# A spectral mixing transform feeding a two-layer expert: the transform in an unbroken turn, its last two batches' inverse kept in DRAM, and the seven-product form of w_out in eleven tiles in place of five

## The chip, the cores and the metric

The kernel runs on one core of a Trainium2 chip. The metric is the device time of one execution in microseconds (us). Three runs of the kernel before gave a median of 2568.8 us (2568.28 to 2569.6).

## What is computed

```python
X = np.fft.rfft(x, axis=1)                      # x: 8 x 3008 x 256
Yr = Xr @ w_r - Xi @ w_i + b_r                  # complex mix of the 256 channels
Yi = Xr @ w_i + Xi @ w_r + b_i
Yr, Yi = softshrink(Yr, 0.01), softshrink(Yi, 0.01)
y = np.fft.irfft(Yr + 1j * Yi, n=3008, axis=1)
h = y.reshape(24064, 256) @ w_in                # 256 x 2048
g = np.maximum(h, 0.0) ** 2
out = g @ w_out                                 # 2048 x 256
```

Everything is float32. The products are done as sums of three products of parts, high by high, low by high and high by low (fp32r), so every product of the algorithm is three matmuls.

## The kernel before

**The expert.** The 24064 tokens are worked in 48 tiles, six to a batch (`tiles`, line 492): tile t belongs to batch t // 6 and has 2h tokens, h being 252 or 250. A tile has eight steps (`Step`, line 690), one for every 256 of the 2048 hidden columns. `first` and `second` (702, 733) make the hidden columns with seven products in place of eight (21 matmuls of h columns, 12 and 9). DVE adds the products up and rectifies them, ACT squares them into `mc` and copies the high part to `mg0`, and POOL subtracts the low part `mg1` in two halves (line 752). `out(0)` and `out(1)` (811) multiply by w_out, two steps later: 6 matmuls of 2h columns each, accumulated over the tile in two PSUM banks `pso`. Only the last two matmuls of each six read `mg1`.

**The seven-product form of w_out.** In tiles named by `FREE` (line 59: 42 to 46) the steps 1, 3 and 5 (`SEVEN`) use seven products for w_out too (`out_seven`, 768): 9 and 12 matmuls of h columns. It needs sums of the hidden columns (`forms`, 755: four on DVE, copies of the high parts on ACT, low parts `ftl` on POOL), sums of w_out made once (`out_sums`, 663, on POOL) and two further PSUM banks of the transform's pair `psf` as accumulators for the rest of the tile; `tile_sums` (678) adds them up on DVE at its end. The memory for this (`LATE`: `wsh`, `wsl`, `tt`, `th`, `tl`, `ts`) lies where the transform of a batch has its tiles (`SIDE`), so `late` (904) opens it once the last batch's forward part and mix are through.

**The transform of the next batches** fills in between the steps. For each batch: 13 `Fwd` (210; short DFTs, stored to DRAM `s1`), 12 `Pair` (267; second DFT, mix, shrink, first inverse stage, stored to `s3`) and 16 `Back` (499; last inverse stage of 188 tokens, 6 matmuls). A `Back` loads its tile `du`, multiplies into two `psf` banks, and ACT and DVE add the two halves into the next tile's raw tokens `yr`. `Tokens` (576) makes the seven sums and low parts `yt` of the tile's tokens, which `first` and `second` read.

**The order of the work** is written by the main loop (1078 to 1131). It counts slots m: step n has slots 2n (`first`) and 2n+1 (`second`); a batch has 96. Transform work hangs on a list of (slot, job): a job is put behind what that slot writes. In the kernel before, the 12 Pairs of a batch stand 6 slots apart in the slots 1 to about 75 of the batch ahead of its use, the 13 Fwd in the slots 4 to 78, and the rest of the 96 has neither. The 16 Backs of a tile's batch run one tile ahead.

A scheduler turns this into one queue per engine, each of which runs in order; earlier written work goes first where it is ready. `then` (572) chains instructions of an engine, so that their order is as written: all matmuls of the steps (`product`, `out`, `out_seven`), DVE's and ACT's parts of the steps, and on POOL the low parts of `mg` and the sums of `Tokens.free`. Loads on SP are chained too (`load_next`, 117). A tile with one buffer (`ts` has one) is given out again only when the last reader of its former holder is done.

**The last batch before the change.** `last_tasks` (897) runs all 16 Backs of batch 7 in the slots 645.5 to 671 of the loop, 1.6 slots apart, with `du` in the tags `th`, `tl`, `th`, `ts` in turn; the last one (q = 15, tag `ts`) loads in slot 666 and multiplies in slot 671. Their results go to DRAM (`y7`), from where `raw_load` (892) brings each tile. The tokens of tile t + 1 are then made inside the steps of tile t in `FREE` by `Tokens.free`, written into the odd slots:

```python
            ahead = k and t in FREE and i in (0, 2, 4, 6)
            if ahead:
                if i == 0:
                    tokens = Tokens(t + 1)
                tokens.free(i, False)
            (steps[n].second if k else steps[n].first)()
```

Its first act is to take the tile `ts` and write two differences into it on POOL (582 to 591), ahead of the low parts of the same step in POOL's chain. For tile 42 that is slot 673.

## Time and profile before

| | |
|---|---|
| median of three runs | 2568.8 us |
| the profiled execution's own time | 2568.52 us |
| its span, first to last instruction | 2566.7 us |
| PE busy | 2557.8 us, 17345 matmuls |
| DVE, POOL, ACT busy | 1864.5, 1711.5, 1405.7 us |
| granted TensorE clock, mean | 1.000 |
| HBM | 96 GB/s over the span |

The profile gives one execution. PE is the matmuls of TensorE, PEld its weight loads, DVE the vector engine, ACT the scalar engine, POOL GpSimd, SP the queue that issues most transfers. Matmuls overlap in the records, each ending after the next has begun, so what one costs is read from start to start. Tile 42 begins at about 2311 us, tile 46 at about 2474 us and the last, 47, at about 2515 us.

### The profile page before, as it was taken

The page shows a single profiled execution, that of the slowest core. Times are in us where ns is not written, and L with a number is a line of the kernel's source. Part 1 is how long each engine was busy: PE and PEld are TensorE (multiplying, and loading weights), DVE is VectorE, ACT ScalarE, POOL GpSimd, SP SyncE. Part 2 cuts the span into 40 slices and gives each one's busy share as a digit, 9 for nine tenths or more (in the row PEclk, how much of TensorE's full clock was granted, in tenths as well). Part 3 has the DMA queues.
Part 4 walks back from the last instruction along what each step waited for, and adds up shares of the span by engine and source line. Part 5 has one row for each costly group of instructions (what it writes and reads, how often), then busy time and mean ns, then how long its engine had stood idle before and what let it go on. Part 6 is the DMA issues. An engine that isn't in the chain of part 4 may idle for free.

```text
span 2566.7 us, 47569 instructions
## 1 busy us (share of the span) xinstructions
PE 2557.8 (100%) x17345; PEld 2361.9 (92%) x17345; DVE 1864.5 (73%) x3727; ACT 1405.7 (55%) x2151; POOL 1711.5 (67%) x1653
## 2 busy tenths in 40 slices
PE   9999999999999999999999999999999999999999
PEld 7899999999999999999999999999999999999998
DVE  7876766777767776687766877677776676667886
ACT  5655555555555555555555555555555455555554
POOL 1167666676767766677667666667777666768885
PEclk9999999999999999999999999999999999999999
DMA  9633332343323333233332333323342223340000
GB/s 313 196 94 90 115 93 83 94 122 106 94 68 106 103 106 96 65 109 103 116 94 70 103 112 109 94 58 113 102 120 76 70 89 103 93 119 31 25 25 17
DMA packets 186608, 249.82 MB, mean 97 GB/s; under 512 B 18616, under 2 KB 131760, under 8 KB 186376
## 3 DMA queue, kind: packets, MB, share of 16 engines
q1 hardware_dynamic: 172961, 221.51, 27.7%
q0 software_dynamic: 13280, 25.16, 4.2%
q8 instruction: 139, 2.28, 0.4%
q14 instruction: 93, 0.76, 0.1%
q10 hardware_dynamic: 135, 0.12, 0.0%
HBM read 146.76 MB, written 99.95 MB: 96 GB/s over the span
## 4 chain that ended last, share of the span: by engine, by line
PE 98%; DVE 1%; DMA 1%; ACT 0%; issue 0%; POOL 0%; SPq 0%; ACTq 0%
PE pso L574 40%; PE psh L574 36%; PE psf L309 7%; PE psf L288 3%; PE psf L342 2%; PE psf L250 2%; PE psf L474 1%; PE psf L552 1%; PE psf L551 1%; PE psf L574 1%; PE psf L548 1%; PE psf L372 1%; PE psf L529 1%; PE psf L409 0%; PE psf L484 0%; PE psf L460 0%
## 5 line engine op out<-in xcount | busy, mean ns | idle before, releaser
L112 POOL TENSOR_TENSOR mg<-mc,mg 128x500 fp32r<-128x500 f32 (+1 forms) x766 | 990.0, 1314 | 485.7 <-ACT mg L108 404.6
L574 PE MATMUL pso<-mg,wout 128*128 128x500 f32 (+2 forms) x4473 | 1128.0, 390 | 0.0
L574 PE MATMUL psh<-yt,win 128*128 128x250 f32 (+1 forms) x8064 | 1070.2, 280 | 0.8 <-DVE mc L574 0.3
L574 PEld LDWEIGHTS psh<-yt,win 128*128 128x128 f32 x8064 | 1018.8, 189 | 29.4 <-DVE yt L112 0.6
L574 PEld LDWEIGHTS pso<-mg,wout 128*128 128x128 f32 x4473 | 798.6, 189 | 126.2
L574 ACT ACTIVATE mc<-mc 128x1000 f32<-128x1000 f32 (+1 forms) x384 | 400.5, 1043 | 494.6 <-DVE mc L574 493.4
L574 DVE CUSTOM_DVE_ANT_0 mc<-psh,mv 128x250 f32<-128x250 f32 (+3 forms) x769 | 418.6, 546 | 336.8 <-PE psh L574 291.6
L108 ACT CAST mg<-mc 128x1000 fp32r<-128x1000 f32 (+1 forms) x385 | 396.7, 1031 | 15.0 <-ACT mc L574 0.4
L574 DVE TENSOR_TENSOR mv<-psh,mu 128x500 f32<-128x500 f32 (+1 forms) x384 | 260.8, 679 | 43.3 <-PE psh L574 8.9
L309 PE MATMUL psf<-wx,kxh 128*128 128x256 f32 x1008 | 209.5, 281 | 0.0
L109 DVE COPY mp<-psh 128x250 f32<-128x250 f32 (+1 forms) x384 | 160.4, 418 | 50.9 <-PE psh L574 27.4
L330 DVE TENSOR_TENSOR kv<-psf,ke 64x256 f32<-64x256 f32 x336 | 141.6, 422 | 46.3 <-PE psf L309 33.5
L221 POOL TENSOR_TENSOR xs<-xt 120x256 f32<-120x256 f32 x156 | 121.2, 798 | 80.0 <-DMA xt<-x_in 41.9
L309 PEld LDWEIGHTS psf<-wx,kxh 128*128 128x128 f32 x1008 | 167.0, 189 | 2.7
L574 DVE TENSOR_TENSOR mu<-psh,mp 128x250 f32<-128x250 f32 (+1 forms) x384 | 160.7, 418 | 12.0
L574 DVE CUSTOM_DVE_ANT_0 mc<-psh,mp 128x250 f32<-128x250 f32 (+1 forms) x384 | 156.9, 408 | 7.1 <-PE psh L574 6.9
L108 ACT COPY dy<-psf 128x188 f32<-128x188 f32 (+2 forms) x229 | 70.2, 317 | 162.4 <-PE psf L552 161.9
L112 POOL TENSOR_TENSOR ksl<-kv,ksh 128x512 fp32r<-128x512 f32 x84 | 109.0, 1297 | 57.7 <-ACT ksh L108 56.2
L309 PE MATMUL psf<-wx,kxl 128*128 128x256 f32 x504 | 141.6, 281 | 0.0
L112 POOL TENSOR_TENSOR yt<-yr,yt 128x250 fp32r<-128x250 f32 (+1 forms) x94 | 88.7, 944 | 46.3 <-ACT yt L108 46.3
L332 ACT ACTIVATE kc<-kv,low 128x512 f32<-128x512 f32 x84 | 60.8, 724 | 100.3 <-DVE kv L330 100.2
L112 DVE TENSOR_TENSOR xl<-xs,xh 120x512 fp32r<-120x512 f32 x78 | 112.4, 1441 | 1.3 <-ACT xh L108 1.3
(163 smaller groups left out, 2883.4 us busy)
## 6 DMA issues: line engine op xcount, KB each, us to landing
du<-s SPq DMA_DIRECT2D x112, 256.0 KB, 2.9
ka<-s SPq DMA_DIRECT2D x96, 256.0 KB, 2.9
kcm<-cm_in POOLq DMA_DIRECT2D x84, 256.0 KB, 3.6
s<-kuh SPq DMA_DIRECT2D x84, 256.0 KB, 2.9
s<-kul SPq DMA_DIRECT2D x84, 256.0 KB, 3.5
s<-xe SPq DMA_DIRECT2D x82, 240.0 KB, 2.4
xt<-x_in SPq DMA_DIRECT2D x81, 240.0 KB, 3.1
out<-mo SPq DMA_DIRECT2D x64, 250.0 KB, 2.3
```

Source lines behind the costliest of these rows:

```text
L108: return act.copy(out=out, in_=in_)
L109: return eng.tensor_copy(out=out, in_=in_)
L112: return eng.tensor_tensor(out=out, in0=a, in1=b, op=ALU.subtract)
L221: return eng.tensor_tensor(out=out[:, :n], in0=self.xt[:, :n, 0], in1=self.xt[:, :n, 1], op=(ALU.add, ALU.subtract)[t])
L250: nc.tensor.matmul(ps[:, t], am_sb[0][:, j, t], v[:, t], start=n == 0, stop=n == 2)
L288: nc.tensor.matmul(pv[:, :, c, g, :], self.a[:, g, c * 128:(c + 1) * 128], bg, start=True, stop=True)
L309: self.last = nc.tensor.matmul(ps, l, wx[j][:, k, c, :], start=n == 0, stop=n == 5)
L330: dve.tensor_add(out=v[64 * r:64 * r + 64, g], in0=ps[gs], in1=self.e[gs, r])
L332: act.activation(r, v, AF.Relu, bias=low)
L342: nc.tensor.matmul(ps[:, g], self.cm[:, g, j * 128:(j + 1) * 128], r[:, g], start=n == 0, stop=n == 2)
L372: self.mm = nc.tensor.matmul(ps[:M1, t], nam if t and i else am32[:, t], self.xt[:, 0, i], start=i == 0, stop=i == 1)
L574: last_of[eng] = op(*args, **kwargs)
```

## The change

`FREE` becomes 36 to 46, and the Backs of batch 6 go to DRAM as those of batch 7 do. The batches from 2 on follow one another every 78 slots (13 turns of 6) from slot 92, in place of every 96: Fwd of batch b + 1 start four slots after batch b's turn, its Pairs seven slots after. All job lists are put together once, in absolute slots. Worked out from the new numbers: the last turn begins in slot 482 and batch 7's Pairs end in 554.25 (`done`); batch 6's Backs run from 488 to 553, 4.2 slots apart, their `du` in the tag `xt`; `late` is in 554.75; batch 7's Backs run from 555.25 to 580.85, 1.6 slots apart as before. The last of them loads in slot 576.05 and multiplies in 580.85. Tile 36 begins in slot 576, and `Tokens.free` for tile 37 first runs in slot 577.

```diff
--- before.py
+++ after.py
@@ -55,7 +55,8 @@
 
 A11, A12, A22, S1, S2, S3, S4 = range(7)
 B11, B21, B22, T1, T3, T2, T4 = range(7)
-ENDS = B - 1
+ENDS = B - 2
+TURN0, TURNS, PACE = 92, J, 6
 FREE = range(ENDS * len(HALF), B * len(HALF) - 1)
 SEVEN = (1, 3, 5)
 
@@ -71,7 +72,7 @@
 
     s3 = [dram.tile([M2 + M2 if b else M2, NP, D], F32, name=f"s3_{b}") for b in range(B)]
 
-    y7 = dram.tile([128, 2, S], F32, name="y7")
+    ys = {b: dram.tile([128, 2, S], F32, name=f"y_{b}") for b in range(ENDS, B)}
 
     am32 = const.tile([M1, 2, M1], F32, name="am32")
     dx_sb = const.tile([128, 2, 4 * N2], F32R, name="dx_sb")
@@ -507,20 +508,25 @@
 
         def load(self):
             tag = "du" if self.spans[0][0] else "mc"
-            if self.b == ENDS:
+            if self.b == B - 1:
                 tag = ("th", "tl", "th", "ts")[self.q % 4]
             ps = slice(2 * self.q, 2 * self.q + 2)
             if self.b == 0:
                 self.u = T("du", [M2, 2, D], F32, tag=tag)
                 load_next(self.u, s3[0][:, ps])
                 return
-            if self.b == ENDS:
-                self.u = T("du", [128, 1024], F32R, tag=tag)[:, :3 * D].rearrange("p (k d) -> p k d", k=3)
+            if self.b == B - 1:
+                u = T("du", [128, 1024], F32R, tag=tag)[:, :3 * D].rearrange("p (k d) -> p k d", k=3)
+                self.u, self.u2 = u[:, :2], u[:, 2]
+            elif self.b >= ENDS:
+                self.u, self.u2 = [T("du", [128, 2, D], F32R, tag="xt") for _ in range(2)]
+                self.u2 = self.u2[:, 0]
             else:
-                self.u = T("du", [128, 3, D], F32R, tag=tag)
-            load_next(self.u[:, :2].bitcast(F32), s3[self.b][:128, ps])
+                u = T("du", [128, 3, D], F32R, tag=tag)
+                self.u, self.u2 = u[:, :2], u[:, 2]
+            load_next(self.u.bitcast(F32), s3[self.b][:128, ps])
             for p in range(2):
-                load_next(self.u[64 * p:64 * p + 64, 2].bitcast(F32), s3[self.b][128:, 2 * self.q + p])
+                load_next(self.u2[64 * p:64 * p + 64].bitcast(F32), s3[self.b][128:, 2 * self.q + p])
 
         def mm32(self):
             ps = bank([128, 512])[:, :2 * W2].rearrange("c (k p t) -> c k p t", k=2, p=2)
@@ -549,17 +555,16 @@
 
                 with tc.issue_after(mm.ins):
                     nc.tensor.matmul(pv[:, :, 1], self.u[:, 1, cs], dx_sb[:, 0], start=False, stop=False)
-                nc.tensor.matmul(ps[:, 0], self.u[:, 2, cs], dx_sb[:, 1], start=False, stop=True)
+                nc.tensor.matmul(ps[:, 0], self.u2[:, cs], dx_sb[:, 1], start=False, stop=True)
                 self.done = copy(act, y[:, c], ps[:, 1])
                 for n, (t, lo, hi, at) in enumerate(self.spans):
-                    kept = t in FREE[1:] or t > FREE[-1]
+                    kept = t >= FREE[0]
                     if n == c == 0 and t not in raw and not kept:
                         raw[t] = T("yr", [128, 2, 2 * HM], F32)
                     o = y[:, c, lo:hi] if n or kept else raw[t][:, c, at:at + hi - lo]
                     self.cut = dve.tensor_add(out=o, in0=ps[:, 0, lo:hi], in1=y[:, c, lo:hi])
-            if self.b == ENDS and self.spans[-1][0] > FREE[0]:
-                lo = min(lo for t, lo, _, _ in self.spans if t > FREE[0])
-                nc.sync.dma_start(y7[:, :, W2 * self.q + lo:W2 * (self.q + 1)], y[:, :, lo:])
+            if self.b >= ENDS:
+                nc.sync.dma_start(ys[self.b][:, :, W2 * self.q:W2 * (self.q + 1)], y)
 
         def put(self):
             t, lo, hi, _ = self.spans[1]
@@ -845,7 +850,7 @@
         jobs = []
         for j, u in enumerate(pairs):
             at = start + j * step
-            if j:
+            if j or u.b > 1:
                 jobs += [(at - 3.7, u.load)]
             jobs += [
                 (at, u.fwd), (at + 1.0, u.sums), (at + 3.7, u.load_back),
@@ -854,21 +859,23 @@
             ]
         return jobs
 
-    def fwd_tasks(b, start, step):
+    def fwd_tasks(b, start):
         jobs = []
-        step0 = (b - 2) * len(HALF) * NF // 2
         for q in range(J):
-            f, at = Fwd(b, q), start + q * step - (step0 > 0 and q == J - 1)
-            add = f.add if q or not step0 else lambda f=f, s=steps[step0 - 1]: later(s.low, f.add)
-            even = 6 * q + (4 if step0 else 14 if q < 4 else 18)
+            f, even = Fwd(b, q), start + PACE * q
+            add = f.add
+            if b > 2 and q == 0:
+                add = lambda f=f, s=steps[(start - 4) // 2 - 1]: later(s.low, f.add)
+            elif b == 2 and q > 3:
+                even += 4
             jobs += [(even - 5.0, f.load), (even - 1.9, add), (even - 0.9, f.split), (even + 0.1, f.lower)]
-            jobs += [(even + (2.0 if step0 else 1.2), f.run)]
+            jobs += [(even + (2.0 if b > 2 else 1.2), f.run)]
         return jobs
 
     def back_tasks(t, start):
         b, c0, h = tiles[t]
         new = range(-(-c0 // W2), -(-(c0 + 2 * h) // W2))
-        if b == ENDS:
+        if b >= ENDS:
             new = ()
         jobs = []
         for j, q in enumerate(new):
@@ -880,6 +887,8 @@
                 jobs += [(start + 14.6, k.put)]
         if t > FREE[0]:
             return [(start, lambda: raw_load(t))]
+        if t == FREE[0]:
+            jobs += [(start, lambda: raw_load(t))]
         k = Tokens(t)
         if t == 0:
             return jobs + [(start + 7.1, k.begin)]
@@ -890,16 +899,16 @@
         return jobs
 
     def raw_load(t):
-        _, c0, h = tiles[t]
+        b, c0, h = tiles[t]
         raw[t] = T("yr", [128, 2, 2 * HM], F32)
-        load_next(raw[t][:, :, :2 * h], y7[:, :, c0:c0 + 2 * h])
-
-    def last_tasks(start, step):
-        jobs = [(start, late)]
+        load_next(raw[t][:, :, :2 * h], ys[b][:, :, c0:c0 + 2 * h])
+
+    def kept_tasks(b, start, step, ahead):
+        jobs = []
         for q in range(S // W2):
-            k = Back(ENDS, q)
-            jobs += [(start + 1.0 + step * max(q - 2, 0), k.load), (start + 2.6 + step * q, k.mm)]
-        return jobs + [(start + 2.0 + 5.0 * j, lambda n=n: out_sums(n)) for j, n in enumerate(SEVEN)]
+            k = Back(b, q)
+            jobs += [(start + step * max(q - ahead, 0), k.load), (start + 1.6 + step * q, k.mm)]
+        return jobs
 
     def late():
         side.close()
@@ -1046,7 +1055,6 @@
 
     pairs = [[Pair(b, j) for j in range(G // 2)] for b in range(B)]
     steps = [Step(t, n) for t in range(len(tiles)) for n in range(NF // 2)]
-    slots = len(HALF) * NF
     first = sorted(back_tasks(0, 0), key=lambda j: j[0])
     kind = {"load": 0, "mm": 1}
     first = [[job for _, job in first if kind.get(job.__name__, 2) == k] for k in range(3)]
@@ -1076,33 +1084,27 @@
         chain[nc.sync] = p.get
 
     jobs = []
+    for q in range(EDGE, J):
+        jobs += [(0.4 + 1.2 * (q - EDGE), second[q].load)]
+        jobs += [(4.0 + 1.2 * (q - EDGE), lambda q=q: behind(second[q].run))]
+    jobs += [(0.6, lambda: part_load(parts[-2])), (2.6, lambda: part_load(parts[-1]))]
+    jobs += [(10.2, pairs[1][0].load), (10.0, load_am)]
+    jobs += pair_tasks(pairs[1], 10.8, 5.25, 9.1)
+    jobs += fwd_tasks(2, 14)
+    for b in range(2, B):
+        start = TURN0 + (b - 2) * TURNS * PACE
+        jobs += pair_tasks(pairs[b], start + PACE + 1.0, PACE if b < B - 1 else 5.25)
+        if b + 1 < B:
+            jobs += fwd_tasks(b + 1, start + 4)
+    for t in range(1, len(tiles)):
+        jobs += back_tasks(t, NF * (t - 1) + 0.5)
+    over = TURN0 + (B - 3) * TURNS * PACE
+    jobs += kept_tasks(B - 2, over + 6.0, 4.2, 0)
+    done = over + PACE + 1.0 + 11 * 5.25 + 7.5
+    jobs += [(done + 0.5, late)] + kept_tasks(B - 1, done + 1.0, 1.6, 2)
+    jobs += [(done + 3.0 + 6.0 * j, lambda n=n: out_sums(n)) for j, n in enumerate(SEVEN)]
+    jobs.sort(key=lambda j: j[0])
     for m in range(2 * len(steps) + 4):
-        b, r = divmod(m, slots)
-        if r == 0 and b < B:
-            jobs = [(t - slots, job) for t, job in jobs]
-            if b + 1 < B:
-                first, step, end = 1.0, 6.0, 7.1
-                if b == 0:
-                    first, step, end = 10.8, 5.25, 9.1
-                    for q in range(EDGE, J):
-                        jobs += [(0.4 + 1.2 * (q - EDGE), second[q].load)]
-                        jobs += [(4.0 + 1.2 * (q - EDGE), lambda q=q: behind(second[q].run))]
-                    jobs += [(0.6, lambda: part_load(parts[-2])), (2.6, lambda: part_load(parts[-1]))]
-                    jobs += [(first - 0.6, pairs[1][0].load), (10.0, load_am)]
-                if b + 1 == ENDS:
-                    step = 5.25
-                    jobs += last_tasks(68.5, 1.6)
-                jobs += pair_tasks(pairs[b + 1], first, step, end)
-            if b + 2 < B:
-                first, step = (2.6, 7.0) if b else (13.6, 6.0)
-                jobs += fwd_tasks(b + 2, first, step) + [(95.0, pairs[b + 2][0].load)]
-            for j in range(len(HALF)):
-                t = b * len(HALF) + j + 1
-                if t < len(tiles) and (j or b == 0):
-                    jobs += back_tasks(t, NF * j + 0.5)
-            if b + 1 < B:
-                jobs += back_tasks((b + 1) * len(HALF) + 1, slots + 0.5)
-            jobs.sort(key=lambda j: j[0])
         n, k = divmod(m, 2)
         if k and 0 <= n - 2 < len(steps):
             steps[n - 2].out(1)
@@ -1127,7 +1129,7 @@
         if m == max(LATER):
             conv.close()
             pools.update(dict.fromkeys(CONV), **dict.fromkeys(SIDE, memory(side, "side")))
-        while jobs and jobs[0][0] < r + 1:
+        while jobs and jobs[0][0] < m + 1:
             jobs.pop(0)[1]()
 
 
```

## Rows read from the trace of the kernel before

**Rows 1.** The page: the span, busy time by engine, the chain that ended last.

```profile
span 2566.7 us, 47569 instructions
PE 2557.8 (100%) x17345; PEld 2361.9 (92%) x17345; DVE 1864.5 (73%) x3727; ACT 1405.7 (55%) x2151; POOL 1711.5 (67%) x1653
...
PE 98%; DVE 1%; DMA 1%; ACT 0%; issue 0%; POOL 0%; SPq 0%; ACTq 0%
```

**Rows 2.** Busy time by stretch: length, then us (instructions) of each engine.

```profile
701.00:746.00 45.00, 45.00 (x298) 41.20 (x297) 27.10 (x60) 23.16 (x33) 26.99 (x27) 1.00 0.24 74
852.00:908.00 56.00, 56.00 (x393) 52.29 (x392) 43.23 (x85) 32.05 (x50) 40.69 (x41) 1.00 0.35 104
2161.00:2216.00 55.00, 55.00 (x383) 51.17 (x383) 39.27 (x83) 29.53 (x46) 33.81 (x33) 1.00 0.32 94
2352.00:2393.00 41.00, 41.00 (x296) 38.59 (x295) 34.70 (x63) 22.00 (x26) 35.35 (x32) 1.00 0.08 27
```

**Rows 3.** Timeline of PE, tile 42 (start, length, count): plain out, then seven-product out.

```profile
2323.48 2.90 PE L574 MATMUL pso<-mg,wout 128*128 128x504 f32 x12
2326.22 2.62 PE L574 MATMUL psh<-yt,win 128*128 128x252 f32 x21
2328.68 0.28 PE L574 MATMUL psf<-mg,wout 128*128 128x252 f32 x1
...
2331.15 2.63 PE L574 MATMUL psh<-yt,win 128*128 128x252 f32 x21
```

**Rows 4.** DMA issues: size and median us from issue to landing.

```profile
du<-s SPq DMA_DIRECT2D x112, 256.0 KB, 2.9
s<-kul SPq DMA_DIRECT2D x84, 256.0 KB, 3.5
...
y<-dy SPq DMA_DIRECT2D x13, 188.0 KB, 2.5
...
yr<-y SPq DMA_DIRECT2D x4, 500.0 KB, 3.9
```

**Rows 5.** Timeline of PE, end of tile 41 and start of tile 42: the last two Backs.

```profile
2307.11 0.25 PE L548 MATMUL psf<-dx_sb,du 128*128 128x188 f32 x1
...
2308.35 0.25 PE L548 MATMUL psf<-dx_sb,du 128*128 128x188 f32 x1
...
2310.02 1.55 PE L574 MATMUL psh<-yt,win 128*128 128x250 f32 x12
2311.41 0.25 PE L548 MATMUL psf<-dx_sb,du 128*128 128x188 f32 x1
...
2318.27 2.90 PE L574 MATMUL pso<-mg,wout 128*128 128x500 f32 x12
```

**Rows 6.** Timeline of POOL, the first three steps of tile 42.

```profile
2316.82 1.43 POOL L112 TENSOR_TENSOR ts<-yr 128x252 f32<-128x252 f32 x2
2320.01 2.51 POOL L112 TENSOR_TENSOR mg<-mc,mg 128x504 fp32r<-128x504 f32 x2 [1.76 <-ACT mg L108]
2322.49 0.72 POOL L574 TENSOR_TENSOR ts<-yr,ts 128x252 f32<-128x252 f32 x1
2323.29 0.75 POOL L112 TENSOR_TENSOR ts<-yr,ts 128x252 f32<-128x252 f32 x1
2325.20 2.66 POOL L112 TENSOR_TENSOR mg<-mc,mg 128x252 fp32r<-128x252 f32 x2 [1.16 <-ACT mg L108]
2327.83 2.70 POOL L112 TENSOR_TENSOR ftl<-ftt,fth 128x504 fp32r<-128x504 f32 x2
```

**Rows 7.** Timelines of ACT and DVE: freeing the bank of the Back at 2307.11.

```profile
2307.62 0.32 ACT L108 COPY dy<-psf 128x188 f32<-128x188 f32 x1 [0.27 <-PE psf L552]
...
2307.97 0.35 DVE L559 TENSOR_TENSOR dy<-psf,dy 128x188 f32<-128x188 f32 x1
```

**Rows 8.** Timeline of PE, tile 46: the seven-product out of step 5, first row and what follows it.

```profile
2491.11 0.28 PE L574 MATMUL psf<-mg,wout 128*128 128x250 f32 x1
...
2494.36 1.90 PE L574 MATMUL psh<-yt,win 128*128 128x250 f32 x15
```

## The prediction

> **What bounds the kernel now.** The page comes first: TensorE is busy for 2557.8 of a span of 2566.7 us, and the chain that ended last is PE for 98% of it [rows 1]. All idle time of PE together is 8.9 us, so a change of order alone can give back little; time goes down where matmuls go away or get shorter, and up where PE is made to wait. The second view is busy time by stretch [rows 2]: a tile with hardly any transform beside it (701 to 746), one in the thick of it (852 to 908), one with batch 7's Pairs at their closer pace of 5.25 slots (2161 to 2216), and a tile of seven-product form (2352 to 2393). PE is busy from end to end in all four, whether DVE has 27.10 of 45 us or 43.23 of 56. The third view is PE's timeline, read from start to start [rows 3, 5]. The profiled execution took 2568.52 us, 0.3 below the median of 2568.8; the sum is made against the former and put on the latter.
>
> **Six more tiles in seven-product form.** Per step the 12 matmuls of 504 columns take 2326.22 - 2323.48 = 2.74 us, 228 ns each, and the 21 of 252 columns take 2331.15 - 2328.68 = 2.47 us, 118 ns each [rows 3]. The saving is 0.27 us in each of 6 x 3 = 18 steps: **-4.9 us**. What comes with it lies on other engines: per step the sums on DVE, copies on ACT and two more subtractions of 2.70 us together on POOL [rows 6], per tile `tile_sums`. A tile that has all this keeps DVE 34.70, POOL 35.35 and ACT 22.00 us of 41 busy, and PE still 41.00 [rows 2]; the cover is PE's own work, thin on POOL (under 6 us a tile). The 3 `out_sums` are the same three, only earlier. [...]
>
> **The transform without pauses.** The same Pairs, Fwds and Backs run, at the 6 slots apart that they have now, only with the pauses taken out. In a pause PE is busy 45.00 of 45 us and in the thick of it 56.00 of 56 [rows 2], so moving matmuls from one to the other changes neither sum: **0**, bounded by the 8.9 us of idle time on the side of a gain. What hides it is that DVE has 43.23 of 56 us there [rows 2]; the new slots 488 to 555, with Pairs 5.25, batch 6's Backs 4.2 and batch 5's 6 slots apart and no Fwd, come nearest to the stretch 2161 to 2216, with 39.27 of 55, which leaves 15.7 for batch 6's adds. If that cover went, PE would wait for DVE to empty its banks. The first Pair's load of each batch moves from slot 95 to 3.3 slots behind the batch's last Fwd, some 9 us at 2.6 us a slot (a step of two slots is 2323.48 - 2318.27 = 5.21 us [rows 3, 5]), and waits on SP for that Fwd's store; behind it stand `du`, `xt` and output stores, and the stores and loads listed land within 3.9 us [rows 4].
>
> **Batch 6 kept in DRAM.** Added: 16 stores for batch 6 and a fuller set for batch 7, 7 more loads of `yr`, 25 or so issues on SP; removed: five small POOL copies. Stores land in 2.5 us and tile loads in 3.9 [rows 4]; tile 36's load is written in slot 560.5 and first read in 567.6, 18 us later. **0**; if it came late, tile 36's first products would.
>
> **Where the last Back now stands.** This is the term that decides. Before, the last Back multiplies in slot 671 and POOL takes its tile's buffer `ts` for tile 43's tokens in slot 673. After, it multiplies in slot 580.85, but `Tokens.free` asks for `ts` in slot 577, four slots earlier, and `ts` has one buffer. POOL runs in order, and its two differences into `ts` are chained ahead of step 288's low parts of `mg`. So these wait for a Back that is written behind step 288's `out(0)`, and the last two of the six matmuls of that `out(0)` read the low parts. PE can't get by: it issues four matmuls, stalls, takes the last Back (it is the only other work ready), and waits for POOL.
>
> The price, with tile 42 as the pattern for tile 36. Today the step's low parts start at 2320.01, the first half done by 2321.3; the matmul that needs it is the fifth after 2323.48, at 2324.4 [rows 3, 6]: 3.1 us in hand. After, POOL starts only behind the Back: two differences 1.43 us and the first half of `mg` 2.51 / 2 = 1.25, plus about 0.3 for the last matmul's end (0.25 us long [rows 5]) and the handing over: **+3.0 us** of idle PE. Next late is step 289, the first seven-product step. From the restart at R, POOL still has 1.25 of `mg`, 0.72 + 0.75 of differences, 2.66 of `mg` and 2.70 of `ftl` [rows 6], to R + 8.1. PE has 8 matmuls of 228 ns, 21 in about 2.45 us, and comes to the last `ftl` 2.2 us into the next out: R + 6.5. So **+1.6 us** more. Afterwards POOL is late by what PE is late. Lower bound: nothing, if the Back is run early enough. Upper: in today's run the Back before the last falls into an `out` as well (2307.11 and 2308.35 [rows 5]), and its bank is free only 1.2 us after it starts (to 2308.32 [rows 7]); if it lies so again, the last Back starts 1.2 us later, for 5.8 in all. I take 4.6, by the durations of the very instructions that will run.
>
> **Sum.** 2568.5 - 4.9 + 0 + 0 + 4.6 = 2568.2, and on the median **2568.5 us**; its own range 2566.5 to 2570.5. A measurement of this kernel can tell about 0.2%, 5.1 us, from no change, so this is no change.
>
> **Rivals.**
> - *The wait does not bite*: the last Back runs before POOL needs `ts`. It would have to run by the time that step 289's `second` is through, about two slots ahead of where it is written. Against it: the last Back of before is written behind the `second` that begins at 2310.02 and runs at 2311.41, after it [rows 5]; earlier written work goes first. For it: nothing chains it. Time: 2568.8 - 4.9 = 2563.9, with 0.25 to 0.3 us a step 2563.4 to 2564.3. Chance 0.2.
> - *The last stage runs late as a whole* (slower): batch 7's first `du` load is written 1.0 slot behind the last Pair's `back`, where it was 3.25 behind. The store of `kul` lands in 3.5 us and `du` in 2.9 [rows 4], over two slots together, so the first Backs are late. If the lateness is worked off over 16 Backs the forecast stands; if it stays, POOL and so PE wait for each slot of it 2.6 us more, and 2.25 slots give 2568.5 + 5.9 = 2574.4. It is slower by over 0.2% from about two slots on. For it: the tightness; against: a bank is free in 1.2 us [rows 7] while the Backs come every 1.6 slots, 4.2 us. Chance 0.09.
> - *Seven products do not pay here* (slower): the forms come late in each of the 18 steps as in tile 46, where the 21 matmuls took 2494.36 - 2491.11 = 3.25 us [rows 8]. 18 x (3.25 - 2.74) = +9.2, so 2578. Against: tile 42 and its 41.00 of 41 us [rows 2]. [...] Chance 0.03.
>
> **How the numbers follow.** The forecast has 0.68. Most of the first rival's 0.2 and of the forecast lies within 5.1 us of before; some half of the former, and a little of the latter if the saving is nearer 0.3 us a step, lies beyond: faster 0.15. Slower: two thirds of the second rival, the third, and a tail: 0.1. Same 0.75. The range, 2563.2 to 2572.0, takes in nearly all of the first rival and the forecast with its bounds, and leaves out the upper half of the others.
>
> **What would show it.** In the changed kernel: seven-product outs in tiles 36 to 41 as well, each near 2.47 us; a gap of PE of some 3 us in the third step's time of tile 36, in an out after its fourth matmul, with `ts` on POOL started by a matmul of `du`; a smaller one two steps on, before `ftl`. POOL's `ts` at tile 36 would start after the last Back, not before it. Right about moving: PE's idle time before tile 36 is unchanged within 2 us. It would be wrong if PE has no gap at tile 36 (first rival), if the last Back comes two or more slots after its place (second), or if gaps stand in the middle of the turns, where I expect none.

## The result and the profile after

The change makes the kernel slower: 2585.97 us (median of 4 runs, 2585.57 to 2587.57) against 2569.2 for the kernel before, run beside it. The ratio is 1.0066, with a 95% interval of 1.0049 to 1.0084. The forecast of no change, 2568.5, and its range up to 2572.0 are both missed. The profiled execution took 2585.84 us.

From the page of the changed kernel, the lines that answer to [rows 1]:

```profile
span 2584.0 us, 48123 instructions
PE 2562.5 (99%) x17507; PEld 2373.1 (92%) x17507; DVE 1906.0 (74%) x3817; ACT 1417.6 (55%) x2175; POOL 1762.3 (68%) x1684
...
PE 97%; DVE 1%; DMA 1%; issue 0%; ACT 0%; SPq 0%; POOL 0%; DVEq 0%; POOLq 0%; ACTq 0%
```

These lines alone would mislead. TensorE's busy time rose by 4.7 us although the steps in seven-product form take less of it, and its idle time rose from 8.9 to 21.5. The view by stretch says why; its columns are those of [rows 2]. The first line is a stretch with ordinary transform work beside the steps, the next two lie in tile 34, then come tiles 34 and 36 whole, three parts of tile 36, and the whole of tile 40:

```profile
1893.00:1948.00 55.00, 55.00 (x376) 50.87 (x375) 39.43 (x88) 28.33 (x45) 29.38 (x27) 1.00 0.32 96
1950.00:1957.00 7.00, 4.48 (x31) 3.69 (x29) 4.58 (x12) 3.58 (x6) 3.62 (x5) 0.98 0.88 258
1957.00:1967.00 10.00, 8.85 (x37) 8.05 (x37) 4.14 (x7) 4.99 (x11) 8.29 (x10) 0.50 0.43 131
...
1950.59:2018.98 68.39, 64.72 (x420) 59.47 (x418) 43.73 (x98) 33.90 (x58) 40.61 (x41) 0.93 0.40 121
2066.51:2126.21 59.70, 51.68 (x345) 47.62 (x343) 36.98 (x82) 27.56 (x46) 34.38 (x31) 0.89 0.30 89
...
2083.00:2087.50 4.50, 1.82 (x12) 1.49 (x12) 2.71 (x10) 2.31 (x7) 0.00 (x0) 0.89 0.77 175
2087.50:2099.00 11.50, 6.88 (x21) 5.71 (x22) 1.68 (x7) 1.57 (x5) 6.29 (x8) 0.50 0.28 95
2099.00:2102.00 3.00, 3.00 (x23) 3.00 (x22) 1.55 (x4) 0.65 (x1) 3.00 (x3) 0.81 0.03 5
...
2247.99:2288.50 40.51, 40.51 (x293) 38.20 (x292) 34.49 (x64) 21.90 (x26) 34.66 (x31) 1.00 0.08 26
```

In two places PE has gaps, and behind the gaps the granted clock is 0.50 (1957 to 1967 and 2087.50 to 2099) and the matmuls that do run take nearly twice as long: those of a Back start 0.21 us apart from 2088.15 to 2088.79, where they stood 0.11 us apart from 2084.02 to 2084.24. That counts as busy, which is how the page's busy time grew. Apart from 1.5 us in tile 32 the picture of [rows 2] stands everywhere else, and tile 40 with its seven products runs as the seven-product tile there did (2352 to 2393, which is tile 43).

**How the loss is measured.** The stall of a tile is taken from PE's timeline: the sum, over its matmuls, of what the distance from one start to the next is above the median of the same line and shape, where that is over 0.03 us. It holds idle time and slow clock together. For all tiles it is 20.3 us before and 42.6 after. Tile 32 has 1.5, tile 34 9.9, tile 36 13.4; no other tile gained more than 0.25 us.

**Tile 36.** PE's timeline (start, length, engine, line, work; in brackets the idle time ahead and what ended it), to be read beside [rows 3, 5]:

```profile
2080.71 0.85 PE L579 MATMUL pso<-mg,wout 128*128 128x504 f32 x3
2081.40 0.25 PE L554 MATMUL psf<-dx_sb,du 128*128 128x188 f32 x1
...
2081.70 0.41 PE L579 MATMUL pso<-mg,wout 128*128 128x504 f32 x1
...
2083.72 0.35 PE L554 MATMUL psf<-dx_sb,du 128*128 128x188 f32 x1 [1.29 <-DVE dy L565]
...
2085.09 0.35 PE L554 MATMUL psf<-dx_sb,du 128*128 128x188 f32 x1 [0.46 <-DVE dy L565]
...
2087.64 0.50 PE L554 MATMUL psf<-dx_sb,du 128*128 128x188 f32 x1 [1.64 <-ACT dy L109]
...
2090.96 0.53 PE L554 MATMUL psf<-dx_sb,du 128*128 128x188 f32 x1 [1.75 <-DVE dy L565]
...
2092.14 0.42 PE L558 MATMUL psf<-dx_sb,du 128*128 128x188 f32 x1
2095.28 3.73 PE L579 MATMUL pso<-mg,wout 128*128 128x504 f32 x8 [2.73 <-POOL mg L113]
2098.81 3.24 PE L579 MATMUL psh<-yt,win 128*128 128x252 f32 x21
2101.89 0.28 PE L579 MATMUL psf<-mg,wout 128*128 128x252 f32 x1
```

And POOL's timeline there, the counterpart of [rows 6]:

```profile
2092.64 1.39 POOL L113 TENSOR_TENSOR ts<-yr 128x252 f32<-128x252 f32 x2 [20.55 <-PE psf L558]
2093.99 2.46 POOL L113 TENSOR_TENSOR mg<-mc,mg 128x504 fp32r<-128x504 f32 x2
...
2099.78 2.51 POOL L113 TENSOR_TENSOR ftl<-ftt,fth 128x504 fp32r<-128x504 f32 x2
```

The place is the forecast one. Four matmuls of an `out` run, the fifth needs the low part of `mg`, and POOL stands ahead of it at `ts`, which the last matmul of a Back gives free. But POOL has waited 20.55 us, and between the fourth matmul (2081.70) and the fifth (2095.28) PE runs **five** Backs, not one. The first has its own start at 2081.40, and each of the other four starts with a gap, because two banks and two `dy` tiles have to be emptied first. ACT's timeline shows that its part was held up by transfers as well, twice by the store of an earlier `dy` and once by a copy of tokens that stood ahead of it in ACT's order:

```profile
2086.78 0.54 ACT L109 COPY dy<-psf 128x188 f32<-128x188 f32 x2 [0.77 <-DMA y<-dy]
2089.46 0.40 ACT L109 CAST yt<-yr 128x252 fp32r<-128x252 f32 x1 [2.15 <-DMA yr<-y]
2090.20 0.53 ACT L109 COPY dy<-psf 128x188 f32<-128x188 f32 x2 [0.34 <-DMA y<-dy]
```

**Tile 34** was not on the list at all. PE's timeline:

```profile
1949.66 1.44 PE L579 MATMUL psh<-yt,win 128*128 128x250 f32 x11
...
1953.79 0.35 PE L554 MATMUL psf<-dx_sb,du 128*128 128x188 f32 x1 [1.34 <-DVE kul L113]
...
1956.67 0.40 PE L558 MATMUL psf<-dx_sb,du 128*128 128x188 f32 x1 [0.96 <-DMA du<-s]
...
1960.89 0.58 PE L310 MATMUL psf<-wx,kxh 128*128 128x256 f32 x1 [0.95 <-ACT kxh L109]
...
1965.46 0.62 PE L579 MATMUL psh<-yt,win 128*128 128x250 f32 x2
```

and POOL's:

```profile
1953.95 0.62 POOL L113 TENSOR_TENSOR ms<-yr 128x250 f32<-128x250 f32 x1 [1.26 <-DVE yr L565]
...
1963.66 1.06 POOL L113 TENSOR_TENSOR yt<-ms,yt 128x500 fp32r<-128x500 f32 x1
```

The steps stop for 14 us (1951 to 1965), for tile 34's tokens. Their raw part comes from Backs of batch 5; POOL takes up their sums at 1953.95, behind DVE's addition of such a Back, and has the last `yt` at 1964.72. Meanwhile PE lives on Pairs and Backs, and the row at 1953.79 names what they quarrel over: a Back waits for a `psf` bank until DVE has read a Pair's `kul` from it. The two share two banks.

**How late the last stage was.** Slots can be counted in PE's timeline by the groups of 12 and 9 `psh`. The last `back` of batch 7's Pairs is written in slot 554.25 and ran in 561; before, it was written in 642.25 and ran in 642. In the changed kernel it is this row:

```profile
2024.48 0.40 PE L343 MATMUL psf<-ksh,kcm 128*128 128x256 f32 x2
```

Batch 7's first Back is written in 556.85 and ran in 566, nine slots late. In slot 580 five Backs were still to run, the ones seen above.

### The profile page after: what moved, and what is told of

It reads as the page before. It is cut to its first block, busy times and chain, and to the rows that moved or that the text cites. A ratio compares the mean times of both kernels' runs of the same rounds, so it can differ in the third digit from the quotient of the medians.

```text
span 2584.0 us, 48123 instructions
## 1 busy us (share of the span) xinstructions
PE 2562.5 (99%) x17507; PEld 2373.1 (92%) x17507; DVE 1906.0 (74%) x3817; ACT 1417.6 (55%) x2175; POOL 1762.3 (68%) x1684
## 4 chain that ended last, share of the span: by engine, by line
PE 97%; DVE 1%; DMA 1%; issue 0%; ACT 0%; SPq 0%; POOL 0%; DVEq 0%; POOLq 0%; ACTq 0%
PE pso L579 38%; PE psh L579 36%; PE psf L310 7%; PE psf L289 3%; PE psf L343 2%; PE psf L251 2%; PE psf L579 2%; PE psf L475 1%; PE psf L558 1%; PE psf L557 1%; PE psf L554 1%; PE psf L373 1%; PE psf L535 1%; PE psf L410 0%; PE psf L485 0%; PE psf L461 0%
## 5 line engine op out<-in xcount | busy, mean ns | idle before, releaser
L579 PE MATMUL pso<-mg,wout 128*128 128x500 f32 (+2 forms) x4311 | 1086.4, 389 | 2.7 <-POOL mg L113 2.7
L579 PEld LDWEIGHTS pso<-mg,wout 128*128 128x128 f32 x4311 | 772.8, 189 | 125.2 <-POOL mg L113 3.0
L579 DVE TENSOR_TENSOR mu<-psh,mp 128x250 f32<-128x250 f32 (+1 forms) x384 | 160.8, 419 | 12.3
L310 PEld LDWEIGHTS psf<-wx,kxl 128*128 128x128 f32 x504 | 95.5, 190 | 2.4 <-DVE kxl L113 0.5
```

Of the source, the lines that this page charges most:

```text
L310: self.last = nc.tensor.matmul(ps, l, wx[j][:, k, c, :], start=n == 0, stop=n == 5)
L579: last_of[eng] = op(*args, **kwargs)
```

## The experiments

Every kernel is an edit of the changed one unless another is named. Windows are from a tile's first matmul to the next tile's; columns as in [rows 2].

**e1_turns_only**: batch 6 stays on chip and `FREE` is 42 to 46 again; the turns stay, and batch 7's Backs stay at 555 to 581.

```diff
-ENDS = B - 2
+ENDS = B - 1
...
-    jobs += kept_tasks(B - 2, over + 6.0, 4.2, 0)
```

> The turns without pauses as in the changed kernel, but batch 6 goes straight into its tiles as before and FREE is 42 to 46 again. Theory A (the continuous turns cost nothing; the loss comes from batch 6's Backs crowded into slots 488 to 553 and what they make late): 2569 us, within 2 us of the kernel before, no stall of PE over 1 us in tiles 30 to 42. Rival C (the unbroken turns cost time themselves): a good part of the 17 us stays, 2575 us or more.

Measured: 2583.52 us, ratio 1.0055 [1.0040, 1.0070]. Tile 34 in the first line, tile 36 in the second:

```profile
1948.56:1998.49 49.93, 49.93 (x341) 46.19 (x340) 34.95 (x73) 27.66 (x41) 34.13 (x34) 1.00 0.25 78
2047.64:2109.40 61.76, 54.40 (x340) 49.42 (x338) 31.00 (x81) 26.70 (x49) 31.54 (x32) 0.89 0.32 95
```

Tile 34 has no gap when batch 6's Backs are not there. But the time is far above the 2569 expected, and the edit does not show the turns alone: batch 7's Backs, 1.6 slots apart, now run among batch 6's ordinary ones, and a new stall of 12.3 us stands in tile 36 and 4.7 in 37. e5 tries the turns without this crowding.

**e2_seven_from_37**: the seven products begin one tile later; batch 6 still goes to DRAM.

```diff
+KEPT = ENDS * 6
 TURN0, TURNS, PACE = 92, J, 6
-FREE = range(ENDS * len(HALF), B * len(HALF) - 1)
+FREE = range(KEPT + 1, B * len(HALF) - 1)
...
-                    kept = t >= FREE[0]
+                    kept = t >= KEPT
...
-        if t == FREE[0]:
+        if t >= KEPT:
             jobs += [(start, lambda: raw_load(t))]
```

> The changed kernel with the seven-product form, and the tokens made inside the steps, one tile later (tiles 37 to 46, so ts is first asked for in slot 593). Theory A: the stall of tile 36, about 13 us, goes to under 1 us and the one of tile 34, about 10 us, stays: 2586 - 13 + 0.8 = 2574 us. If the stall of tile 36 came from the load on the engines there and not from the late Backs, it moves to tile 37 and the time stays near 2586.

Measured: 2574.82 us, ratio 1.0024 [1.0014, 1.0033]. Tiles 34 and 36:

```profile
1950.62:2018.38 67.76, 63.42 (x419) 58.06 (x418) 43.92 (x98) 33.71 (x58) 40.61 (x41) 0.95 0.41 122
2065.91:2113.17 47.26, 47.26 (x317) 43.36 (x316) 28.90 (x73) 23.95 (x40) 29.15 (x26) 1.00 0.39 112
```

One tile of seven products less, worth 0.8 us by the forecast's own rate, and the time falls by 11. Tile 36 has lost its gaps, tile 34 keeps 9.2 us: the two losses come apart.

**e3_no_ts**: the four Backs of batch 7 that use `ts` load into the tag `xt`, so POOL's claim of `ts` waits for no Back.

```diff
-            if self.b == B - 1:
+            if self.b == B - 1 and self.q % 4 < 3:
                 u = T("du", [128, 1024], F32R, tag=tag)[:, :3 * D].rearrange("p (k d) -> p k d", k=3)
```

> The changed kernel, but the four Backs of batch 7 that loaded into ts load into the tag xt, so nothing but the tokens ever holds ts. Rival B (the claim on the one buffer ts is the whole cause at tile 36): the stall of tile 36 is gone, 2573 us. Theory A (the Backs are nine slots late when the stage begins and four late at slot 580): they still hold tl, th and the two psf banks when the first seven-product step wants them, so part of the stall stays, 4 to 9 us: 2577 to 2582 us.

Measured: 2580.81 us, ratio 1.0047 [1.0032, 1.0062]. Tile 36:

```profile
2065.78:2121.14 55.36, 50.44 (x345) 47.03 (x344) 36.02 (x82) 27.66 (x46) 34.93 (x31) 0.91 0.33 95
```

Of 13.4 us of stall 9.1 stay without the wait for `ts`. POOL's timeline shows that the tile is still taken late:

```profile
2087.11 1.40 POOL L113 TENSOR_TENSOR ts<-yr 128x252 f32<-128x252 f32 x2 [15.76 <-issue]
```

and SP's, what it now waits for, the load of tile 37's raw tokens, queued behind the `du` of the late Backs:

```profile
2080.20 2.51 SPq L120 DMA_DIRECT2D du<-s  x4
2082.81 0.57 SPq L120 DMA_DIRECT2D yr<-y  x1
```

A load of this size takes 4.4 us here in the median, so it lands about when POOL starts. e15 and e16 move this load.

**e4_own_chain**: the loads of batch 6's Backs leave the chain of loads on SP and get one of their own.

```diff
+            key = "kept" if self.b == ENDS else None
-            load_next(self.u.bitcast(F32), s3[self.b][:128, ps])
+            load_next(self.u.bitcast(F32), s3[self.b][:128, ps], key=key)
...
```

> The changed kernel, but batch 6's loads of du have a chain of their own on SP, so that they no longer stand between the loads of batch 7's Pairs and batch 5's Backs. Rival D (the lateness in slots 488 to 560 comes from loads queued behind a load that waits for its buffer): Pairs and Backs come on time, the stall of tile 34 goes and that of tile 36 shrinks below 5 us: 2566 to 2570 us. Theory A with the two psf banks as the narrow place: no more than 4 us gained, 2582 to 2586 us.

Measured: 2584.78 us, ratio 1.0063 [1.0046, 1.0080]; stalls of 9.0 us in tile 34 and 12.9 in 36. The place of batch 6's loads in SP's queue is not the cause.

**e5_turns_alone**: e1, with batch 7's Backs put back into the slots 645.5 to 671, where they were before. Of the change only the turns are left.

```diff
-ENDS = B - 2
+ENDS = B - 1
...
-    jobs += kept_tasks(B - 2, over + 6.0, 4.2, 0)
     done = over + PACE + 1.0 + 11 * 5.25 + 7.5
+    done = 644.5
-    jobs += [(done + 0.5, late)] + kept_tasks(B - 1, done + 1.0, 1.6, 2)
+    jobs += [(done, late)] + kept_tasks(B - 1, done + 1.0, 1.6, 2)
```

> The unbroken turns alone, cleaner than the first run: batch 6 straight into its tiles, and batch 7's sixteen close-set Backs in slots 645.5 to 671 as before, where nothing else of the transform runs. Theory A, put more sharply (what costs is two streams of Backs in the same slots beside the Pairs or beside each other, not the turns): 2568 to 2570 us, no tile with over 1 us of stalls. Rival C (the turns cost themselves): 2573 us or more.

Measured: 2566.41 us, ratio 0.9990 [0.9981, 1.0000]. Tile 34:

```profile
1949.51:1999.71 50.20, 50.20 (x343) 46.50 (x342) 35.12 (x74) 27.75 (x42) 33.92 (x34) 1.00 0.25 79
```

No tile behind the first has a stall above 0.7 us. The turns cost nothing and may give 2.4 us; the interval ends at no change.

**e6_pairs_six and e7_both_slower**: as e2, with `FREE` from 38 and batch 7's Pairs 6 slots apart in place of 5.25; in e7 batch 6's Backs are 5.0 slots apart in place of 4.2 as well.

```diff
-        jobs += pair_tasks(pairs[b], start + PACE + 1.0, PACE if b < B - 1 else 5.25)
+        jobs += pair_tasks(pairs[b], start + PACE + 1.0, PACE)
...
-    jobs += kept_tasks(B - 2, over + 6.0, 4.2, 0)
-    done = over + PACE + 1.0 + 11 * 5.25 + 7.5
+    jobs += kept_tasks(B - 2, over + 6.0, 5.0, 0)
+    done = over + PACE + 1.0 + 11 * PACE + 7.5
```

(The two lines with `kept_tasks` in e7 alone.)

> Seven products from tile 38, and batch 7's Pairs 6 slots apart in place of 5.25; batch 6's Backs stay 4.2 apart. If the Pairs' closer pace makes tile 34 late, its stall goes: 2565 to 2567 us (3.3 us of four more seven-product tiles gained). If batch 6's Backs make it late whatever the Pairs do, 5 to 9 us of stall stay in tile 34: 2570 to 2575 us.

> As the run before it, and batch 6's Backs 5.0 slots apart in place of 4.2. By theory A crowding is what costs, so with both paces eased no tile has over 1.5 us of stalls: 2565 to 2567 us, faster than either kernel. If the loss is not crowding but batch 6's way through DRAM as such, 2572 us or more.

Measured: e6 2571.77 us, ratio 1.0011 [1.0002, 1.0021], 7.8 us of stall in tile 34; e7 2567.58 us, ratio 0.9996 [0.9987, 1.0006], 1.2 us in tile 34 and 2.4 in 35. Tile 34 of e7:

```profile
1948.98:2003.42 54.44, 53.68 (x372) 49.72 (x370) 39.12 (x85) 29.80 (x47) 32.84 (x32) 1.00 0.35 108
```

Slowing the Pairs alone leaves most of the loss, and slowing both streams takes most of it away. e7 still missed its expectation, by 0.6 us of time and with 2.4 us in tile 35. Its profiled execution took 2569.62 us, 2 us more than the median, and has 2.5 us of stall in tile 17 as well, far from the crowded slots.

**e8_backs_slower**: `FREE` from 39, Pairs at 5.25 as in the change, batch 6's Backs 6.0 slots apart, batch 7's behind them.

```diff
-    jobs += kept_tasks(B - 2, over + 6.0, 4.2, 0)
+    jobs += kept_tasks(B - 2, over + 6.0, 6.0, 0)
     done = over + PACE + 1.0 + 11 * 5.25 + 7.5
+    done = over + 6.0 + 16 * 6.0 + 1.0
```

> Seven products from tile 39, Pairs of batch 7 at 5.25 as in the changed kernel, but batch 6's Backs 6.0 slots apart, and batch 7's Backs behind them. If batch 6's Backs at 4.2 are the excess, the stall of tile 34 goes below 1.5 us and the time is 2565.5 to 2567.5 us (2.5 us of three more seven-product tiles gained). If the Pairs' pace is the excess, 4 us or more of stalls stay: 2570 us or more.

Measured: 2574.75 us, ratio 1.0022 [1.0013, 1.0032]; 8.5 us in tile 34. The slower Backs alone do not help as long as the Pairs come at 5.25. In the kernel before, the Pairs ran at this pace too, without gaps [rows 2], but with one stream of Backs beside them, not two.

**e9_backs_in_turn and e12_three_early**: the Pairs at 5.25; only six (e9) or three (e12) of batch 6's Backs beside them, the others behind the Pairs, 1.6 slots apart in the tags of `LATE`, then batch 7's. `FREE` from 38. The lines of e12 that set the order:

```diff
-    jobs += kept_tasks(B - 2, over + 6.0, 4.2, 0)
     done = over + PACE + 1.0 + 11 * 5.25 + 7.5
-    jobs += [(done + 0.5, late)] + kept_tasks(B - 1, done + 1.0, 1.6, 2)
+    jobs += kept_tasks(B - 2, over + 10.0, 14.0, 0, 0, 3)
+    jobs += [(done + 0.5, late)] + kept_tasks(B - 2, done + 1.0, 1.6, 2, 3)
+    jobs += kept_tasks(B - 1, done + 22.8, 1.6, 2)
```

> Unbroken turns and seven products from tile 38. Six of batch 6's Backs stand 10 slots apart beside batch 7's Pairs (slots 494 to 546), the other ten follow the Pairs at 1.6 slots, then batch 7's sixteen, so that never more than one close-set stream runs; the last multiplies in slot 598, ts is asked for in 609. Theory A (three streams in the same slots make the Backs late): no tile from 30 on with over 1.5 us of stalls, 2566.4 for the turns alone less 4 x 0.85 = 2563 us, 2562 to 2565. If batch 6's way through DRAM costs by itself, 2567 us or more.

> As the run with ten of batch 6's Backs behind the Pairs, but only the three that tile 36 needs stand beside batch 7's Pairs (slots 492 to 520) and thirteen follow. By theory A the stall that was left in tile 34, 3.4 us, goes below 1 us: 2565.8 - 2.5 = 2563.3 us, 2562 to 2564.5. If the stall of 3.4 us has another cause than Backs beside Pairs, nothing changes: 2565.5 us or more.

Measured: e9 2565.81 us, ratio 0.9989 [0.9980, 0.9998], with 3.4 us left in tile 34, over the 1.5 us expected at most; e12 **2562.95 us, ratio 0.9979 [0.9970, 0.9988]**, 5.7 us faster than the kernel before and 23 faster than the change. Tile 34 of e9 and of e12:

```profile
1946.93:2004.92 57.99, 55.71 (x383) 51.34 (x382) 38.98 (x85) 30.21 (x49) 36.05 (x37) 1.00 0.29 87
1950.10:2000.84 50.74, 50.74 (x348) 47.03 (x347) 37.63 (x76) 27.87 (x41) 32.09 (x31) 1.00 0.25 76
```

No tile of e12 behind the first has more than 0.6 us of stall. Its gain agrees with the turns' 2.4 us and four more tiles of seven products than before the change, 4 x 3 x 0.27 = 3.2: 5.6 together.

**e10_no_kept_loads and e11_no_kept_work**: two cuts into e2. In e10 only the first of batch 6's 16 Backs loads its rows and the others multiply these; in e11 they load, but their matmuls, copies and additions are left out and the loaded rows are stored.

```diff
+                if self.q:
+                    self.u, self.u2 = one[0]
+                    return
...
+            if self.b == ENDS:
+                nc.sync.dma_start(ys[self.b][:, :, W2 * self.q:W2 * (self.q + 1)], self.u[:, :, :W2].bitcast(F32))
+                return
```

(The first three lines are e10's, in `load`; the others e11's.)

> The run with seven products from tile 37 (its tile 34 stalls for 9.2 us), but batch 6's sixteen Backs all work on the rows that the first one loaded: 15 x 3 loads left out, so batch 6's result is not the transform's. If the loads (their buffers in xt, their place on SP) make the rest late, the stall of tile 34 goes below 2 us; if it is the two psf banks and the work on PE, ACT and DVE, 6 us or more stay.

> The same run with the counterpart left out: batch 6's Backs load and store as before, but their six matmuls, copies and additions are gone and the loaded rows are stored in their place, so they take no psf bank. By theory A with the banks as the narrow place the stall of tile 34 goes below 1.5 us; the time also falls by PE's own 16 x 6 x 0.105 = 10 us for the matmuls left out. If the loads were the cause, 6 us or more of stall stay.

Measured, one run each: e10 2571.53 us, with tile 34 unchanged:

```profile
1949.58:2017.38 67.80, 63.68 (x419) 58.83 (x418) 44.15 (x99) 33.88 (x58) 40.59 (x41) 0.92 0.31 93
```

e11 2552.68 us, with no stall in tile 34:

```profile
1948.87:1998.80 49.93, 49.93 (x341) 46.19 (x339) 34.96 (x73) 27.66 (x41) 34.11 (x34) 1.00 0.33 102
```

So the stall of tile 34 comes from what the Backs do on the engines and banks, not from their loads and stores. The loads may not be free elsewhere: e10 is 3.3 us below e2, and 1.0 us of that is there when tile 34 begins.

**e13_engines_no_banks and e14_matmuls_alone**: the parts of that work, each alone, again in e2. In e13 batch 6's matmuls are gone and ACT and DVE do their copies and additions from the loaded rows; in e14 the matmuls into `psf` stay, ACT's and DVE's part is gone, and the loaded rows are stored.

```diff
+            if self.b == ENDS:
+                v = self.u[:, :, :W2].bitcast(F32)
+                for c in range(2):
+                    copy(act, y[:, c], v[:, c])
+                    for _, lo, hi, _ in self.spans:
+                        dve.tensor_add(out=y[:, c, lo:hi], in0=v[:, c, lo:hi], in1=y[:, c, lo:hi])
...
                 nc.tensor.matmul(ps[:, 0], self.u2[:, cs], dx_sb[:, 1], start=False, stop=True)
+                if self.b == ENDS:
+                    continue
```

(The first six lines are e13's, the last three e14's.)

> The kernel of e2 with batch 6's last inverse stage cut down: its matmuls and their banks are left out, and ACT's copies and DVE's additions, of the same shapes and in the same number, read the loaded rows in their place; loads and stores stay. If it is the work that ACT and DVE do for batch 6's Backs, or the two buffers of their results, that makes batch 7's Pairs late, tile 34 keeps 6 us or more of the 9.2 us of stall of e2. If it is the two banks of psf, or PE's matmuls, that the Backs share with the Pairs, less than 1.5 us of stall is left and the time is 2568.8 less the saving of nine tiles less the matmuls left out, as in e11: 2551 to 2555. I hold the banks for it.

> The counterpart of e13 and again the kernel of e2: batch 6's Backs keep their matmuls into the banks of psf, ACT's copies and DVE's additions of them are left out, and the loaded rows are stored in place of the results. If the matmuls and the mere number of banks taken in turn make the Pairs late, tile 34 keeps most of its 9.2 us. If it is the time that a bank is held until ACT and DVE have emptied it (1.2 us before the change, longer after it), the banks come free at once here, less than 2 us is left, and the time is 2564 to 2567. If ACT's and DVE's work alone is at fault (e13 then keeps 6 us), less than 2 us is left here too. I expect less than 2 us.

Measured, one run each: e13 2554.44 us, tile 34:

```profile
1949.52:1999.34 49.82, 49.82 (x341) 46.11 (x339) 37.80 (x76) 27.66 (x43) 32.92 (x31) 1.00 0.31 96
```

e14 2566.78 us, tile 34:

```profile
1951.73:2011.05 59.32, 56.97 (x399) 52.90 (x397) 38.49 (x80) 29.10 (x45) 37.12 (x36) 1.00 0.37 111
```

ACT's and DVE's work in itself is refuted: with all of it left in, tile 34 has no gap. e14 missed its expectation: with the banks free as soon as they are written, 3.1 us of stall stay in tile 34 and 1.5 come in 35, against 9.2 in e2. So PE's matmuls and the turns that these Backs take at `psf` are about half of it, and the time that a bank is held until ACT and DVE come to it the other half, with the lower clock in that half alone (0.95 in e2, 1.00 here).

**e15_raw_own and e16_raw_own_no_ts**: tile 36 again. The loads of the raw tokens `yr` get a chain of their own on SP, so that they pass the `du` loads; e15 is the change with this edit, e16 is e3 with it.

```diff
-        load_next(raw[t][:, :, :2 * h], ys[b][:, :, c0:c0 + 2 * h])
+        load_next(raw[t][:, :, :2 * h], ys[b][:, :, c0:c0 + 2 * h], key="raw")
```

> The changed kernel with the same edit alone: the raw tokens' loads in a chain of their own, ts still used by batch 7's Backs. POOL's claim of ts then waits for the last Back as before, whatever the load does, so by the theory of two waits one behind the other tile 36 keeps 11 to 13.4 us of stall and the time is 2583 to 2586. If the load alone were at fault, the stall would be under 6 us and the time under 2579.

> The kernel of e3 with one more edit: the loads of the raw tokens (the tile yr) leave the chain of loads on SP and get one of their own, so that tile 37's load no longer stands behind the du loads of batch 7's last Backs. In e3 POOL's first difference into ts still waited 15.76 us, until 2087.11, and SP issued that load at 2082.81, behind du. If this queue is what is left of the stall in tile 36, it falls from 9.1 us to under 3 and the time from 2580.8 to 2573 to 2576. If it is the late Backs' hold on the two banks of psf and on th and tl, 6 us or more stay and the time is above 2577. I expect the former.

Measured, one run each: e15 2585.40 us, 12.2 us of stall in tile 36, as expected; e16 2581.45 us, 7.6 us, where under 3 were expected. POOL is on time in e16:

```profile
2071.51 1.42 POOL L113 TENSOR_TENSOR ts<-yr 128x252 f32<-128x252 f32 x2
2076.03 2.51 POOL L113 TENSOR_TENSOR mg<-mc,mg 128x504 fp32r<-128x504 f32 x2 [3.10 <-ACT mg L109]
```

PE runs both plain `out`s through and is stopped in the step behind them, ahead of the first seven-product `out`:

```profile
2085.86 0.65 PE L580 MATMUL psh<-yt,win 128*128 128x252 f32 x4
...
2087.60 0.35 PE L555 MATMUL psf<-dx_sb,du 128*128 128x188 f32 x1 [0.78 <-DVE dy L566]
...
2090.20 0.32 PE L555 MATMUL psf<-dx_sb,du 128*128 128x188 f32 x1 [1.17 <-ACT dy L109]
...
2091.97 0.53 PE L555 MATMUL psf<-dx_sb,du 128*128 128x188 f32 x1 [0.85 <-DVE dy L566]
...
2093.76 0.58 PE L580 MATMUL psf<-mg,wout 128*128 128x252 f32 x1 [0.20 <-DVE dy L566]
```

That `out` takes both `psf` banks as accumulators, and it is given them behind the last Back, once DVE has read that one's bank. So three waits stand one behind another in tile 36, `ts` on POOL, the token load on SP and the banks on PE; each is on a Back that is still open, and taking one away only brings the next to light. In e2, where tile 37's tokens are not made by this path and the seven products come a tile later, all three are gone.

## Why the prediction was wrong

**Where the loss lies.** Start from 2569.2. The seven products take 4.9 off and the turns 2.4; tile 34 adds 9.9 and tile 36 13.4: 2585.2, or 2586.7 with tile 32's 1.5. Measured are 2585.97.

**Six more tiles in seven-product form: right.** Tiles 37 to 41 take 40.5 to 40.7 us each, start to start, and in tile 40 (2247.99 to 2288.50, in the view by stretch) PE is busy from end to end.

The sum for e12, which uses 0.27 us a step, gives 5.6 us where 5.7 were measured. The rival by which seven products do not pay does not show in these tiles. The prediction calls the tile of [rows 2] tile 42; it is tile 43, and nothing hangs on that.

**The transform without pauses: right**, 0 forecast and 2.4 us of gain at most (e5), within the 8.9 us named as its bound.

**Batch 6 kept in DRAM: this step failed first.** It was costed at 0, on the stores, loads and issues, and the cover named, in the term on the transform, was DVE's spare 15.7 us. Loads and stores cost little (e4 is 1.2 us below the change, e10 3.3 below e2) and did not make tile 34 late, and DVE was no limit (in e13 PE is busy for all 49.82 us of tile 34). The two `psf` banks were named only as what a busy DVE would fail to empty; how many turns two streams need at two banks was not worked out. 16 more Backs at 4.2 slots beside Pairs at 5.25, with batch 5's Backs still running, take turns at them, and a Back of tile 34 waited 1.34 us for one (the row at 1953.79). The stretch of before that stood for it, 2161 to 2216 [rows 2], had the same Pairs but one stream of Backs. Price: 9.9 us in tile 34, and Pairs that end 7 slots late.

**Where the last Back now stands: the mechanism right, the size wrong.** `ts`, POOL's order, the fourth and fifth matmul of step 288's `out(0)`: all as written. The terms of the first stall hold as well. From the last Back's last matmul (2092.14) to the restart (2095.28) are 3.1 us, against 0.3 + 1.43 + 1.25 = 3.0. What failed is "takes the last Back (it is the only other work ready)": five Backs were open, and PE spent 2081.40 to 2092.14 on them, with banks, `dy` tiles and the clock against it. And behind `ts` two more waits on the same Backs lay hidden (e3, e16), so that an early `ts` alone would not have saved the forecast. So 4.6 became 13.4. The knock-on of 1.6 before `ftl` did not come: `ftl` is done at 2102.3 and the seven-product `out` that needs it begins at 2101.89 without a gap, since PE itself was slow there: the 21 matmuls of 252 columns ahead of it took 2101.89 - 2098.81 = 3.08 us, against 2.47 in [rows 3].

**The rivals.** "The last stage runs late as a whole" was the right one, at a chance of 0.09 and 2574.4. Its lateness was bounded by 2.25 slots, from the `du` load being written closer to the last Pair. It was nine, because the Pair itself was late, and 16 Backs worked off only part of it. That bound was tied to a place in the written order, with no lateness of what stands ahead, so no price of this rival came near the measured time. The sign set for it, a last Back two or more slots after its place, did not show: the last Back is written in slot 580.85 and ran in 580, since the steps that count the slots stood still while five Backs ran. The other two fell: PE did wait, and seven products pay.

**What was to show it**: PE's idle time before tile 36 was to be unchanged within 2 us. It is not (tile 34 alone has 68.39 - 64.72 = 3.7 us), and that mark, set down for the transform's part, is the one that names the first fault.

**What stays open.** Whether the 2.4 us of the turns are real. Whether PE's time or the banks' turns make e14's half: no run parted these, since every run that has the matmuls of batch 6's Backs has their turns at `psf` as well, and a third bank for `psf` wasn't tried. What batch 5's Backs add: they stand in every run. And e10, e11 and e13 to e16 are one run each.

## What to carry to other kernels

When a second stream of work is moved beside a first one, count the buffers they take turns in (here two PSUM banks), not only the busy shares: engines with a quarter of their time free (DVE was busy for 39.43 of the 55 us from 1893 to 1948) did not keep 16 small jobs from costing 10 us. When an in-order engine claims a buffer of a stage, the price may be not that of the last job of the stage but of all jobs of it still open (here five, 13.4 us where 4.6 were forecast for one), so ask how late the stage is at its start, follow that back through whatever feeds it, and look for a second and third claim behind the first. And a stage that fits before and behind another, if not beside it, may be worth moving: with three Backs beside the Pairs, thirteen behind them and the seven products begun two tiles later, a loss of 17 us became a gain of 6.

## What the runs showed of the hardware

In tiles 34 and 36 gaps cost more than their length. In tile 36 PE had gaps of 1.29, 0.46 and 1.64 us, with PE busy for 1.82 of the 4.50 us to 2087.50; the granted clock fell near the end of that stretch (1.00 from 2083 to 2086, 0.50 from 2086.50 on, 0.89 in the mean) and was 0.50 for the 11.5 us to 2099, and it was coming back (0.81) in 2099 to 2102, with PE busy throughout. In tile 34 PE was busy for 4.48 of 7.00 us ahead of the fall, and the clock was 0.50 for 10 us after it. At 0.50 the 504-column matmuls of tile 36 (2095.87 to 2098.81) come every 0.42 us, where [rows 3] have 0.228. Of the 13.4 us of stall in tile 36 idle time makes 59.70 - 51.68 = 8.0 (the tile's line in the view by stretch). So some 5 us are put down to matmuls at the lower clock, an estimate by what is left, and in the same way some 6 of 9.9 in tile 34, where idle time makes 68.39 - 64.72 = 3.7. What brings the clock down, and after how much idle time, the runs do not show. In e9 and e14, with 2.3 us of idle time in tile 34, the granted clock was 1.00 over the tile, and the stall there was 3.4 and 3.1 us.
